# A chunked linear-attention kernel with a gated output: backward-scan decays, a Sigmoid gate, two products interleaved on opposite tiles, compact loads issued by ScalarE, no filler matmuls

## The chip, the core and the metric

One core of one Trainium2 chip runs the whole program. The metric is the device time of one execution in microseconds (us). The engines are TensorE (PE; its weight loads are listed as PEld), VectorE (DVE), ScalarE (ACT), GpSimd (POOL) and SyncE (SP). Each has its own stream of instructions and runs it in order; semaphores join the streams.

## The reference

All data are float32. There are 4 batches of 8 heads (32 units), 768 steps, head size 40. The state of a unit is a 40x40 matrix with a decay per step and column:

```
for t in range(S):
    y[:, :, t] = np.einsum('bhd,bhde->bhe', rt, state)
    Sa = np.einsum('bhde,bhe->bhd', state, at)
    state_decay = state * wt[:, :, None, :] - np.einsum('bhd,bhe->bhde', Sa, bt)
    state = state_decay + np.einsum('bhd,bhe->bhde', vt, kt)
```

The rows `y` of one step form a vector `x` of 320 numbers. A causal depthwise convolution of 5 taps over time and a sigmoid give a gate; the result is `(gate * (x @ w_val)) @ w_out`.

## The kernel before, in words

**Tiling.** Time is cut into 12 chunks of 64 steps. A tile such as `at` or `k` holds all 32 units of a chunk: the 40 components of a unit lie on partitions 0 to 39 or 64 to 103 (one parity of heads each), 16 units lie side by side, 64 steps each.

**`prep(c)`** makes the running product of the decays, `lam`, with one scan on VectorE over 1040 columns (16 units of 1 + 64; `ind` restarts the scan at each unit). Its inverse comes from Ln and Exp on ScalarE and one Newton step on VectorE (`nw0`, `nw1`, L401 and L403). `at` is multiplied by `lam`; `k` and `b` by the inverse (L406). Then come TensorE's products B-A (`mb_`, 32 matmuls, L412) and A-K (`ma_`, the same line), and the turning of `b` and `k` (L418). B-A is copied for the triangular solve (`lst0` L425, `mb` L426 on ScalarE, `lst1` L428 on VectorE), A-K is masked into `ak` (L432). The A-K products use 2 of the 4 tiles of 64x64 that TensorE's array is cut into (rows and columns of one half), the B-A products all 4.

**`tri(g)`** inverts 32x32 triangles of two chunks at once on VectorE: a transpose (L443), 60 dependent steps (L449, L452), a mask (L456), a diagonal, two transposes `dt` and `dd` (L458, L459). **`solve(c)`** joins the halves: two stages of 32 matmuls of 32x32 (`sx` L471, `sy` L477), whose moving operand is every 32nd number of `dd` or `dt`; L479 copies the triangles into `tt`, and `tt1` (L483, VectorE) adds the result of `sy`. **`gv(c)`** makes the R-V products (L494, 2 x 16 matmuls, on the other two tiles) and masks them into `mv`.

**`chain(c, hf)`** is what goes from chunk to chunk, for two halves of the units: `u0` (L511, L513), `u` (L525, L527), `g` (L538), `ys` (L552 to L556, which gives the outputs and the new state), `z` (L573), with a copy or a product by ScalarE or VectorE behind each. **`moe(c)`** is the gate and the two dense layers: GpSimd moves `y` into `xt`, ScalarE and VectorE make the convolution (L624, L628), five instructions make the sigmoid (Abs, Exp, Ln L632 to L634, L635 on VectorE, Exp L636), TensorE makes `val` (L82, L90) and `out` (L100).

**Order.** `Plan` holds every piece with an engine, an assumed duration and its dependences; a list scheduler (`order`) turns them into one fixed order for each engine, which the code then emits. At run time no engine passes over an instruction that waits. SyncE issues all loads. `k`, `b` and `w` have one buffer each, so a load waits until the chunk before has been read.

**Fillers.** While emitting, the code looks at the planned gaps of TensorE and puts dummy matmuls there (L702, 64x72 from the tile `dm`, results not read): 521 in the program. Each float32 matmul of the program appears in the trace as two, so 1042 there.

Of the kernel before, what the change touches and what calls it, by code (L numbers as in the profile page):

```python
# [109 lines left out]
def moe_steps(nc, mo, pp, wts, wz, xe, xt, store):  # L110
# [159 lines left out]
def dve(n):  # L270
    return 110 + 1.05 * n
# [6 lines left out]
def fast_path(ctx, tc, ins, out, nch, cst, wts, wz, wmx):  # L278
# [13 lines left out]
    W = new("w", [ER, P16, C + 1])  # L292
# [3 lines left out]
    Y0 = new("y0", [ER, P16, C])  # L296
# [11 lines left out]
    DD = new("dd", [128, 32, 32])  # L308
    MX = new("mx", [128, 32, 32])
# [13 lines left out]
    dm = new("dm", [128, 72])  # L323
# [7 lines left out]
    m01 = [cst[:, 224 + i:225 + i] for i in range(2)]  # L331
    plan = Plan()
# [36 lines left out]
    def load(c):  # L369
        n = c % NA  # L370
        op(("ldw", c), "SP", 700, lambda: dma(W, ins["w"][c]), w=["w"], lat=2500)
        op(("lda", c), "SP", 700, lambda: dma(AT[n], ins["a"][c]), w=[("at", n)], lat=2500)
        for x, nm in enumerate("kb"):
            op(("ld" + nm, c), "SP", 700, lambda x=x, nm=nm: dma(KB[x], ins[nm][c]), w=[nm], lat=2500)

    def load2(c):
        op(("ldvp", c), "SP", 700, lambda: dma(VP, ins["vp"][c]), w=["vp"], lat=2500)
        op(("ldvt", c), "SP", 700, lambda: dma(VT, ins["vt"][c]), w=["vt"], lat=2500)

    def load3(c):  # L380
        n = c % 2
        op(("ldrg", c), "SP", 700, lambda: dma(RG[n], ins["rg"][c]), w=[("rg", n)], lat=2500)
        op(("ldri", c), "SP", 700, lambda: dma(RI[n], ins["ri"][c]), w=[("ri", n)], lat=2800)
        op(("ldmv", c), "SP", 700, lambda: dma(MV[n], ins["mv"][c]), w=[("mv", n)], lat=2800)

    def prep(c):

        n, g = c % NA, bof[c]
        lam, at, wv = LAM[n], AT[n], W[:, :, 1:C + 1]
        lm = lam[:, :, 1:C + 1]  # L390
        op(("scan", c), "DVE", 2750, lambda: V.tensor_tensor_scan(
            out=lam.rearrange("p u t -> p (u t)"), data0=W.rearrange("p u t -> p (u t)"),
            data1=ind.rearrange("p u t -> p (u t)"), initial=0.0, op0=ALU.mult, op1=ALU.max), r=["w", "ind"], w=[("lam", n)])
# [465 lines left out]
```

## Time and profile before

| | us |
|---|---|
| median of 3 runs (630.28, 630.94, 681.89) | 630.94 |
| the profiled execution's own time | 626.14 |
| its span (first to last instruction) | 624.0 |
| TensorE busy / weight loads busy | 516.8 / 456.4 |
| VectorE busy | 422.2 |
| ScalarE busy | 223.8 |
| mean granted TensorE clock | 0.83 of 2.4 GHz |

The busy time is the union of an engine's instructions; TensorE's matmuls are pipelined, so a busy TensorE need not be at its peak. The granted clock is 1.0 (2.4 GHz) or 0.5 (1.2 GHz) at any moment; a figure between is the mean over a stretch. The chain of waits follows the work back from the last instruction, at each step to what released it.

Three stretches are spoken of. Up to about 115 us the first chunks are prepared, and the first `u` starts at 115.3 us. From 115 to 545 us all kinds of work run side by side. From 545 us on the preparations are over, and only the last chunks' chains and dense layers are left.

### The profile page before, as it was taken

The numbers are of one execution on the slowest core, as the hardware profiler recorded it, in microseconds if no ns is written. First come the engines' busy times: TensorE is split into PE (matmuls) and PEld (weight loads), VectorE is DVE, ScalarE is ACT, GpSimd is POOL, SyncE is SP. The second block draws the span as 40 slices with busy tenths as digits, with TensorE's granted clock in tenths as the row PEclk, the third lists the DMA queues.
The fourth block names the chain that finished last, engine by engine and source line by source line (L and its number), as shares of the span: only waits on it lengthen the run. The fifth ranks groups of instructions, "written<-read, shape, count | busy, mean of one in ns | idle before, by whom it ended". The sixth has DMA issues, their size and how long they took to land.

```text
span 624.0 us, 29668 instructions
## 1 busy us (share of the span) xinstructions
PE 516.8 (83%) x13715; PEld 456.4 (73%) x13715; DVE 422.2 (68%) x924; ACT 223.8 (36%) x362; POOL 74.9 (12%) x151
## 2 busy tenths in 40 slices
PE   0577889686968899878979898999899986999981
PEld 0577888586967778867877887878688885797760
DVE  6397886975883758666775868689969784342430
ACT  3114443231713423523446343455344232432230
POOL 1000000030021000300020203002030312021300
PEclk9996879777785857976986979699979897598986
DMA  8973314144054551245452636341532435001100
GB/s 209 288 180 107 91 45 107 51 141 99 3 158 114 134 163 60 54 129 160 131 149 57 175 82 185 99 126 54 164 91 74 127 95 154 23 15 32 28 22 25
DMA packets 22149, 65.59 MB, mean 105 GB/s; under 512 B 4420, under 2 KB 8508, under 8 KB 22020
## 3 DMA queue, kind: packets, MB, share of 16 engines
q1 hardware_dynamic: 14292, 55.51, 32.3%
q0 software_dynamic: 4608, 4.19, 2.6%
q10 hardware_dynamic: 3120, 3.93, 1.9%
q8 instruction: 109, 1.79, 1.2%
q14 instruction: 20, 0.16, 0.1%
HBM read 55.51 MB, written 3.93 MB: 95 GB/s over the span
## 4 chain that ended last, share of the span: by engine, by line
PE 66%; DVE 12%; DMA 10%; issue 9%; ACT 2%; SPq 0%; POOL 0%; ACTq 0%; DVEq 0%; POOLq 0%
PE pm L100 8%; PE pc L702 7%; PE pp L412 6%; PE pm L82 6%; PE pp L418 5%; PE px L471 4%; DMA b<-in_b 3%; PE px L477 3%; PE px L494 3%; PE pc L538 3%; PE pc L552 3%; PE pc L513 3%; PE pc L554 3%; PE pc L556 3%; PE pc L511 2%
## 5 line engine op out<-in xcount | busy, mean ns | idle before, releaser
L619 POOL DMA_DIRECT2D xt<-xe x144 | 73.1, 515 | 511.6 <-DVE x L452 143.3
L702 PE MATMUL pc<-dm 128*64 128x72 f32 x1042 | 94.4, 253 | 7.0 <-DVE pc L366 4.1
L702 PEld LDWEIGHTS pc<-dm 128*64 128x64 f32 x1042 | 83.4, 158 | 14.5 <-issue 5.5
L628 DVE SCALAR_TENSOR_TENSOR ag<-xt,wts,ag 128x256 f32<-128x256 f32 (+1 forms) x144 | 60.2, 437 | 14.6 <-ACT ag L624 14.6
L449 DVE TENSOR_TENSOR tm<-x 128x30 f32<-128x30 f32 (+14 forms) x210 | 68.7, 327 | 1.4
L452 DVE TENSOR_TENSOR x<-x,tm 128x30 f32<-128x30 f32 (+14 forms) x210 | 68.6, 327 | 1.3
L100 PE MATMUL pm<-wts,ag 128*128 128x320 f32 x144 | 61.1, 552 | 0.0
L554 PE MATMUL pc<-mv,kt 64*40 64x104 f32 x768 | 43.1, 259 | 2.6 <-issue 2.6
L552 PE MATMUL pc<-ri,zd 40*40 40x104 f32 x704 | 40.8, 265 | 3.6 <-issue 2.4
L100 PEld LDWEIGHTS pm<-wts,ag 128*128 128x128 f32 x144 | 27.9, 222 | 21.3 <-issue 16.7
L494 PE MATMUL px<-rg,vt 40*64 40x64 f32 x768 | 30.6, 235 | 15.4 <-DMA rg<-in_rg 15.4
L556 PE MATMUL pc<-mu,bt 64*40 64x104 f32 x768 | 42.1, 258 | 0.0
L494 PEld LDWEIGHTS px<-rg,vt 40*64 40x64 f32 x768 | 27.9, 149 | 17.4 <-issue 16.9
L406 DVE TENSOR_TENSOR b<-b,y 104x1024 f32<-104x1024 f32 x12 | 14.7, 1225 | 36.8 <-DMA b<-in_b 36.8
L525 PE MATMUL pc<-tt,u 64*40 64x64 f32 x768 | 30.9, 241 | 9.6 <-DVE tt L483 5.8
L513 PE MATMUL pc<-vp,ak 64*64 64x40 f32 x768 | 35.2, 272 | 1.9 <-issue 1.9
L525 PEld LDWEIGHTS pc<-tt,u 64*40 64x40 f32 x768 | 27.7, 131 | 12.2 <-DVE tt L483 5.9
L511 PE MATMUL pc<-st,at 40*64 40x40 f32 x704 | 32.7, 269 | 3.3 <-issue 3.3
L395 ACT ACTIVATE y<-w,bias 104x1024 f32<-104x1024 f32 x24 | 27.6, 1150 | 21.6 <-DMA w<-in_w 16.6
L412 PE MATMUL pp<-at,k 40*64 40x64 f32 x768 | 29.5, 239 | 6.1 <-DVE lst L428 3.4
L82 PE MATMUL pm<-xt,wts 128*128 128x128 f32 x192 | 34.4, 307 | 0.0
L425 ACT ACTIVATE lst<-pp,cst 128x512 f32<-128x512 f32 x12 | 13.9, 1160 | 55.9 <-PE pp L412 55.9
(104 smaller groups left out, 1070.9 us busy)
## 6 DMA issues: line engine op xcount, KB each, us to landing
mv<-in_mv SPq DMA_DIRECT2D x12, 832.0 KB
ri<-in_ri SPq DMA_DIRECT2D x12, 676.0 KB
w<-in_w SPq DMA_DIRECT2D x12, 422.5 KB
at<-in_a SPq DMA_DIRECT2D x12, 416.0 KB
b<-in_b SPq DMA_DIRECT2D x12, 416.0 KB
k<-in_k SPq DMA_DIRECT2D x12, 416.0 KB
vt<-in_vt SPq DMA_DIRECT2D x12, 416.0 KB
rg<-in_rg SPq DMA_DIRECT2D x12, 416.0 KB
```

The source lines that it names most:

```text
L82: T.matmul(out=ps[:, j * 2 * L:(j + 1) * 2 * L], lhsT=x[:, m * 128:m * 128 + 128], rhs=xt[:, q:q + 2, 4:4 + L], start=(k == 0), stop=(k == 2))
L100: T.matmul(out=ps, lhsT=gv[r, q * L:q * L + 128], rhs=wo[k][r], start=(k == 0), stop=(k == 2))
L412: T.matmul(out=PP[rows(a, 64), s, q * C:q * C + C], lhsT=KB[x][rk, 2 * q + s], rhs=at[rk, 2 * q + s], start=True, stop=True)
L449: V.tensor_tensor(out=tv, in0=XS[:, j + 1:32, j:j + 1].to_broadcast([128, n, j]), in1=XS[:, j:j + 1, 0:j].to_broadcast([128, n, j]), op=AL ...
L452: V.tensor_tensor(out=XS[:, j + 1:32, 0:j], in0=XS[:, j + 1:32, 0:j], in1=tv, op=ALU.subtract)
L494: T.matmul(out=PX[rows(a, 64), (4 * s + q) * C:(4 * s + q + 1) * C], lhsT=VT[r, m], rhs=RG[n][r, m], start=True, stop=True)
L552: T.matmul(out=o, lhsT=ZD[r, m], rhs=RI[v][r, m], start=True, stop=False)
L554: T.matmul(out=o, lhsT=KBT[0][k][r, m], rhs=MV[v][r, m], start=not c, stop=False)
L556: T.matmul(out=o, lhsT=KBT[1][k][r, m], rhs=MU[r, m], start=False, stop=True)
L619: G.dma_start(out=o, in_=x)
L628: op(("cv", c, j, k), "DVE", 90 + 1.05 * nn[k], lambda k=k, q=q, j=j: V.scalar_tensor_tensor(out=acc[:, q], in0=xt[:, q, j:j + C], scalar= ...
L702: T.matmul(out=f[0:64, 0, 440:512], lhsT=dm[:, 0:64], rhs=dm, start=True, stop=True)
```

## The change

- `prep`: Ln, Exp and the two Newton instructions go. A second scan runs backward over the same columns and gives the inverse decay times the chunk's total decay inverse, which is put into `ind` by a reciprocal of 16 columns; a memset restores `ind`. `b` is now made ahead of `k`.
- `lst`: the tile's layout is turned, so that three ScalarE copies (two of them on 32 partitions) write it in rows; `begin` now reads with a stride. The mask of `tri` moves into `dc`, one VectorE instruction per pair of chunks, which also turns the layout, so that `sx` and `sy` read rows. `dd` is transposed per chunk from `dc`. `tt1` becomes two ScalarE copies.
- `akgv(c, d)`: A-K of chunk c and R-V of chunk d alternate matmul by matmul on the four tiles. In the loop c is three chunks and d one chunk ahead of the chain. Ten calls have both; two have A-K alone, two R-V alone. `turn` holds what stood in `prep`.
- The gate is one Sigmoid; the activation table loaded at the start is another.
- `val`: 4 matmuls in place of 6 for the same columns (two of 256, two of 128).
- Loads of `vp`, `vt`, `rg`, `mv`, `ri` go from SyncE to ScalarE's queue. `mv` and `ri` are stored without their constant parts (832 to 320 KB, 676 to 416 KB) and land in pieces of 160 and 256 bytes; the identity in `ri` is loaded once per buffer.
- The fillers go. The assumed durations of the plan are changed, and so the order of everything.

The core of the diff (plan durations and host layouts are left out):

```diff
-            for k in range(3):
-                x = wv[k + j if k == 2 else k]
-                q = 8 if k == 2 else 4 * k + 2 * j
...
+        for k in range(2):
+            T.matmul(out=ps, lhsT=wv[k][:, m * 128:m * 128 + 128], rhs=xt[:, 4 * k:4 * k + 4, 4:4 + L], start=(k == 0), stop=False)
...
+    def dma2(o, i):
+        A.dma_start(out=o, in_=i)
...
-        op(("ldri", c), "SP", 700, lambda: dma(RI[n], ins["ri"][c]), w=[("ri", n)], lat=2800)
-        op(("ldmv", c), "SP", 700, lambda: dma(MV[n], ins["mv"][c]), w=[("mv", n)], lat=2800)
+        op(("ldmv", c), "ACT", 560, lambda: dma2(MV[n][:, :, C:RW], ins["mv"][c]), w=[("mv", n)], lat=LD)
+            op(("ldri", c), "ACT", 560, lambda: dma2(RI[n][:, :, 0:C], ins["ri"][c]), w=[("ri", n)], lat=LD)
...
-        op(("ln", c), "ACT", act(1024), lambda: A.activation(out=Y0, in_=lm, func=AF.Ln), r=[("lam", n)], w=["y0"])
-        op(("exp", c), "ACT", act(1024), lambda: A.activation(out=Y0, in_=Y0, func=AF.Exp, scale=-1.0), w=["y0"])
...
+        op(("rc", c), "DVE", 200, lambda: V.reciprocal(out=ind[:, :, C], in_=lm), r=[("lam", n)], w=["ind"])
+        op(("scab", c), "DVE", 2240, lambda: V.tensor_tensor_scan(
+            out=back(flat(Y0)), data0=back(WF[:, 1:P16 * (C + 1) + 1]), data1=back(flat(ind)), initial=0.0, op0=ALU.mult, op1=ALU.max),
+           r=["w", "wpad", "ind"], w=["y0"])
...
+        for x in range(2):
+            def go(x=x):
+                for q in range(8):
+                    for par in range(2):
+                        if c is not None:
+                            r = rows(par, D)
+                            T.matmul(out=PP[rows(par, 64), 0, q * C:q * C + C], lhsT=KB[0][r, 2 * q + x], rhs=AT[n][r, 2 * q + x], start=True, stop=True)
+                        if d is not None:
+                            m, r = 8 * (q // 4) + 4 * x + q % 4, rows(1 - par, D)
+                            T.matmul(out=PP[rows(par, 64), 1, q * C:q * C + C], lhsT=VT[r, m], rhs=RG[v][r, m], start=True, stop=True)
...
+        op(("dc", g), "DVE", 1150, lambda: V.tensor_tensor(
+            out=DC, in0=DT.rearrange("p t m -> p m t"), in1=maskD.unsqueeze(1).to_broadcast([128, 32, 32]), op=ALU.mult), r=["dt", "cst"], w=["dc"])
...
-        op(("tt1", c), "DVE", dve(512), lambda: V.scalar_tensor_tensor(
-            out=TT[n][:, :, 32:64], in0=pv, scalar=m01[0], in1=TT[n][:, :, 32:64], op0=ALU.mult, op1=ALU.add), r=pxb + ["cst"], w=[("tt1", n)])
+        for i in range(2):
+            lo = slice(64 * i, 64 * i + 32)
+            op(("tt1", c, i), "ACT", act(512), lambda lo=lo: A.copy(out=TT[n][lo, :, 32:64], in_=pv[lo]), r=pxb, w=[("tt1", n)])
...
-        op(("gln", c), "ACT", act(640), lambda: A.activation(out=gt, in_=gt, func=AF.Ln, bias=1.0), w=["gv"])
+        op(("gate", c), "ACT", act(640), lambda: A.activation(out=acc, in_=acc, func=AF.Sigmoid), w=ak)
...
-                for i in range(k):
-                    T.matmul(out=f[0:64, 0, 440:512], lhsT=dm[:, 0:64], rhs=dm, start=True, stop=True)
```

**The order at three places.** First, TensorE's stream at its very start. Before (L494 is R-V of chunk 0, L412 its B-A and A-K products, L702 fillers):

```order
L702 MATMUL pc_121<-dm 64x72 x5
L494 MATMUL px<-rg_86,vt 64x64 x16
L702 MATMUL pc_121<-dm 64x72 x8
L412 MATMUL pp<-at_71,b 64x64 x32
L702 MATMUL pc_121<-dm 64x72 x12
```

And now (L417 is B-A, L437 A-K, L440 R-V):

```order
L417 MATMUL pp<-at_71,b 64x64 x32
L437 MATMUL pp<-at_71,k 64x64
L440 MATMUL pp<-rg_87,vt 64x64
L437 MATMUL pp<-at_71,k 64x64
L440 MATMUL pp<-rg_87,vt 64x64
```

R-V, which needs the loads of `rg` and `vt`, stood ahead of B-A and now stands behind it.

Second, TensorE's stream in the middle of the program. Before (the rows that the trace shows from 389 to 402 us; L573 is `z`, L418 the turning of `b` and `k`):

```order
L494 MATMUL px<-rg_87,vt 64x64 x16
L702 MATMUL pc_121<-dm 64x72
L412 MATMUL pp<-at_72,k 64x64 x32
L573 MATMUL pc_121<-cst,st 40x40 x16
L573 MATMUL pc_122<-cst,st 40x40 x16
L702 MATMUL pc_121<-dm 64x72 x8
L418 MATMUL pp<-cst,b 64x40 x32
L702 MATMUL pc_122<-dm 64x72 x5
L418 MATMUL pp<-cst,k 64x40 x32
```

And now, at a like place (L95 is `out`, L500 and L503 are `sx` and `sy`):

```order
L417 MATMUL pp<-at_71,b 64x64 x32
L95 MATMUL pm<-wts,ag 128x320 x3
L500 MATMUL px<-dd,mb 32x32 x32
L95 MATMUL pm<-wts,ag 128x320 x3
L503 MATMUL px<-dc,xx 32x32 x32
L437 MATMUL pp<-at_71,k 64x64
L440 MATMUL pp<-rg_87,vt 64x64
```

The separate runs of L494 and of L412 from `k` have become one alternating run, and no dummy stands between stages.

Third, the end of the first solve. Before, VectorE's stream (L47 to L54 convert the weights, L449 and L452 are steps of `tri`, L483 is `tt1`):

```order
L51 TENSOR_SCALAR xt<-xt 128x323
L449 TENSOR_TENSOR tm<-x 128x240
L52 SCALAR_TENSOR_TENSOR wts<-xt 128x323
L452 TENSOR_TENSOR x<-x,tm 128x16x15
L483 SCALAR_TENSOR_TENSOR tt_105<-px,cst,tt_105 128x16x32
L449 TENSOR_TENSOR tm<-x 128x240
```

And now ScalarE's stream (L502 copies `xx`, L498 fills `tt` from `dc`, L425 copies `mb`, L507 is `tt1`, L538 the copy of `ut`):

```order
L502 COPY xx<-px 128x512
L498 ACTIVATE tt_106<-dc,cst 128x16x32
L425 COPY mb<-pp 128x512
L507 COPY tt_106<-px 32x16x32
L498 ACTIVATE tt_106<-dc,cst 128x16x32
L507 COPY tt_106<-px 32x16x32
L538 COPY ut_110<-pc_121 104x512
```

The last step before the first `u` has left VectorE's stream of weight conversions and triangle steps.

## Rows read from the trace of the kernel before

**Rows 1.** The three stretches: start and end, length, busy us and instructions of each engine, mean granted clock, share of the DMA engines, GB/s.

```profile
0.00:115.00 115.00, 75.26 (x1666) 71.65 (x1666) 85.28 (x171) 36.22 (x48) 1.88 (x7) 0.88 0.52 142
115.00:545.00 430.00, 379.91 (x10694) 334.46 (x10698) 313.11 (x700) 167.73 (x277) 60.93 (x120) 0.81 0.40 110
545.00:624.00 79.00, 61.64 (x1367) 50.32 (x1360) 23.78 (x55) 19.85 (x37) 12.13 (x24) 0.87 0.09 24
```

**Rows 2.** The fillers' instructions alone (L702) in the same middle stretch and in four stretches within it: busy us of PE and of PEld, granted clock, DMA share, GB/s.

```profile
115.00:545.00 430.00, 39.83 (x358) 33.05 (x358) 0.81 0.40 110
337.00:357.00 20.00, 0.00 (x0) 0.00 (x0) 1.00 0.52 140
365.00:395.00 30.00, 0.82 (x6) 0.53 (x7) 0.96 0.56 160
395.00:408.00 13.00, 4.57 (x34) 3.92 (x34) 0.50 0.43 113
425.00:457.00 32.00, 2.02 (x26) 1.57 (x24) 1.00 0.46 134
```

**Rows 3.** The chain of waits in the stretch from 115 to 545 us, by line, as shares of that stretch.

```profile
by line: issue 10.3%; PE pm L100 9.8%; PE pc L702 7.6%; PE pm L82 7.3%; PE pp L412 7.1%; PE pp L418 5.7%; PE px L471 4.6%; PE px L477 4.5%; PE px L494 4.3%; PE pc L538 4.2%; DMA b<-in_b 4.0%; PE pc L513 3.6%; PE pc L552 3.6%; PE pc L511 3.4
```

**Rows 4.** What VectorE waited for from 115 to 545 us: us in all, times, longest.

```profile
DVE b L406 <- DMA b<-in_b: 31.6, 5, 9.5
DVE tt L483 <- PE px L477: 30.8, 6, 10.7
...
DVE lst L428 <- ACT mb L426: 2.2, 3, 1.1
```

**Rows 5.** Pieces of the chain of waits between 384 and 404 us: start, length, what.

```profile
394.93 2.01 PE pc L702 x16
396.93 1.88 PE pp L418 x64
398.81 1.39 PE pc L702 x10
```

**Rows 6.** The product stages (L412 alone) in three short stretches, columns as in Rows 2: A-K at 2.4 GHz, A-K at 1.2 GHz, B-A at 2.4 GHz.

```profile
125.30:127.20 1.90, 1.90 (x64) 1.86 (x64) 1.00 0.47 75
160.00:163.60 3.60, 3.60 (x64) 3.46 (x64) 0.50 0.02 5
102.00:103.10 1.10, 1.10 (x64) 0.99 (x64) 1.00 0.79 201
```

**Rows 7.** One `sx` stage (L471 alone) at 2.4 GHz and one at 1.2 GHz, columns as in Rows 2.

```profile
419.40:421.40 2.00, 1.98 (x64) 1.82 (x64) 1.00 0.31 94
323.50:325.60 2.10, 2.02 (x64) 1.88 (x64) 0.50 0.96 245
```

**Rows 8.** Groups of VectorE's instructions by line: busy us, mean ns of one, idle before them.

```profile
L391 DVE TENSOR_TENSOR_SCAN lam<-w,ind 104x1040 f32<-104x1040 f32 x12 | 27.9, 2323 | 1.1 <-DMA w<-in_w 1.1
L403 DVE SCALAR_TENSOR_TENSOR y<-w,y 104x1024 f32<-104x1024 f32 x12 | 14.6, 1219 | 0.0
L428 DVE SCALAR_TENSOR_TENSOR lst<-pp,cst,lst 128x512 f32<-128x512 f32 x12 | 14.0, 1166 | 12.1 <-ACT mb L426 12.1
L459 DVE STREAM_TRANSPOSE dd<-x 128x1024 f32<-128x1024 f32 x7 | 13.7, 1951 | 0.0
L635 DVE SCALAR_TENSOR_TENSOR ag<-ag 128x640 f32<-128x640 f32 x12 | 9.9, 823 | 7.3 <-ACT ag L634 7.3
L443 DVE STREAM_TRANSPOSE x<-lst 128x1024 f32<-128x1024 f32 x7 | 8.8, 1253 | 0.0
L456 DVE TENSOR_TENSOR x<-x,mx 128x1024 f32<-128x1024 f32 x7 | 8.5, 1217 | 0.0
```

**Rows 9.** The DMA queues of SyncE (q1) and ScalarE (q10): packets, MB, the time of the packets as a share of 16 engines' span; and two stretches in which TensorE stood idle (busy us of PE, PEld, DVE, ACT, POOL, granted clock, DMA share, GB/s).

```profile
q1 hardware_dynamic: 14292, 55.51, 32.3%
...
q10 hardware_dynamic: 3120, 3.93, 1.9%
...
182.00:187.20 5.20, 0.21 (x7) 0.07 (x4) 3.19 (x6) 0.00 (x0) 3.50 (x7) 0.63 0.89 247
516.00:522.50 6.50, 1.07 (x74) 0.95 (x70) 4.11 (x13) 0.43 (x1) 2.70 (x6) 0.91 0.87 246
```

**Rows 10.** The timeline at the start of the program and ahead of the first `u`.

```profile
15.39 1.23 DVE L406 TENSOR_TENSOR b<-b,y 104x1024 f32<-104x1024 f32 x1
21.00 1.97 PE L494 MATMUL px<-rg,vt 40*64 40x64 f32 x32 [15.39 <-DMA rg<-in_rg]
25.01 1.75 PE L412 MATMUL pp<-at,b 40*64 40x64 f32 x64
...
96.93 1.98 PE L477 MATMUL px<-dt,xx 32*32 32x32 f32 x64
114.49 0.74 DVE L483 SCALAR_TENSOR_TENSOR tt<-px,cst,tt 128x512 f32<-128x512 f32 x1
```

**Rows 11.** Pieces of the chain of waits in the last gate and behind it.

```profile
597.48 0.75 ACT ag L632
601.41 0.77 DVE ag L644 x2
...
603.25 0.91 PE pc L702 x6
```

**Rows 12.** The timeline of ScalarE's queue: the issue of one transfer (start, length).

```profile
305.44 0.52 ACTq L651 DMA_DIRECT2D out<-xt  x1
```

More of the change, by code (lines that the diff above doesn't have):

```diff
@@ L386, in prep @@
+        if c < 2:
+            op(("eye", c), "SP", 400, lambda: dma(RI[n][:, :, C:RW], ins["eye"]), w=[("rj", n)], lat=LD)
+        if c:
+            op(("ldri", c), "ACT", 560, lambda: dma2(RI[n][:, :, 0:C], ins["ri"][c]), w=[("ri", n)], lat=LD)
     def prep(c):
         n, g = c % NA, bof[c]
[L389 to L393, printed above, removed]
@@ L405, in prep, with flat @@
-        for x, nm in enumerate("kb"):
-            op((nm + "t", c), "DVE", 90 + 1.05 * 1024, lambda x=x: V.tensor_tensor(out=KB[x], in0=KB[x], in1=Y0, op=ALU.mult), r=["y0"], w=[nm])
-        def products(x, far):
+        lam, at, wv, lm, y = LAM[n], AT[n], W[:, :, 1:C + 1], LAM[n][:, :, C], Y0[:, :, 1:C + 1]
+        def flat(x):
+            return x.rearrange("p u t -> p (u t)")
+        op(("scan", c), "DVE", 2240, lambda: V.tensor_tensor_scan(
+            out=flat(lam), data0=flat(W), data1=flat(ind), initial=0.0, op0=ALU.mult, op1=ALU.max), r=["w", "ind"], w=[("lam", n)])
@@ L409, in products @@
+        op(("ic", c), "DVE", 60, lambda: V.memset(ind[:, :, C:C + 1], WLO ** C), w=["ind"])
+        op(("at", c), "DVE", 65 + 1.05 * 1024, lambda: V.tensor_tensor(out=at, in0=at, in1=lam[:, :, 0:C], op=ALU.mult), r=[("lam", n)], w=[("at", n)])
+        for x, nm in ((1, "b"), (0, "k")):
+            op((nm + "t", c), "DVE", 65 + 1.05 * 1024, lambda x=x: V.tensor_tensor(out=KB[x], in0=KB[x], in1=y, op=ALU.mult), r=["y0"], w=[nm])
+        def products():
             for q in range(8):
                 for par, s in UNITS:
-                    rk, a = rows(par, D), par ^ s if far else par
@@ L412, in products @@
-                    T.matmul(out=PP[rows(a, 64), s, q * C:q * C + C], lhsT=KB[x][rk, 2 * q + s], rhs=at[rk, 2 * q + s], start=True, stop=True)
+                    rk = rows(par, D)
+                    T.matmul(out=PP[rows(par ^ s, 64), s, q * C:q * C + C], lhsT=KB[1][rk, 2 * q + s], rhs=at[rk, 2 * q + s], start=True, stop=True)
+        ps = PP.rearrange("p s (q t) -> p (s q) t", t=C)
+        op(("mb_", c), "PE", 1160, products, r=["b", ("at", n)], w=ppb)
+        m0 = g[1] * P16
+        op(("lst", c, 0), "ACT", act(512), lambda: A.copy(out=LST[:, m0:m0 + P16], in_=ps[:, :, 0:32]), r=ppb, w=["lst"])
@@ L442, in flat @@
             return x.rearrange("p a b -> p (a b)")
-        op(("begin", g), "DVE", 1250, lambda: V.transpose(out=flat(XS), in_=flat(LST)), r=["lst"], w=["x"])
+        op(("begin", g), "DVE", 1900, lambda: V.transpose(out=flat(XS), in_=LST.rearrange("p m t -> p t m")), r=["lst"], w=["x"])
         def step(j, half):
@@ L468, in between @@
             for m in range(P16):
                 for a in range(2):
-                    lo, hi = slice(a * 64, a * 64 + 32), slice(a * 64 + 32, a * 64 + 64)
-                    T.matmul(out=PX[hi, m * 32:m * 32 + 32], lhsT=MB[lo, k + m], rhs=DD[lo, :, o + m], start=True, stop=True)
-        def last():
-            for m in range(P16):
-                for a in range(2):
-                    lo, hi = slice(a * 64, a * 64 + 32), slice(a * 64 + 32, a * 64 + 64)
-                    T.matmul(out=PX[lo, m * 32:m * 32 + 32], lhsT=XX[hi, m], rhs=DT[hi, :, o + m], start=True, stop=True)
+                    fn(m, slice(a * 64, a * 64 + 32), slice(a * 64 + 32, a * 64 + 64), slice(m * 32, m * 32 + 32), a)
@@ L486, in gv @@
[L486 to L498 removed]
+        op(("sy", c), "PE", 1300, lambda: quad(lambda m, lo, hi, o, a: T.matmul(out=PX[lo, o], lhsT=XX[hi, m], rhs=dc[hi, m], start=True, stop=True)),
+           r=["dc", "xx"], w=pxb)
@@ L500, in chain @@
+        for i in range(2):
+            lo = slice(64 * i, 64 * i + 32)
+            op(("tt1", c, i), "ACT", act(512), lambda lo=lo: A.copy(out=TT[n][lo, :, 32:64], in_=pv[lo]), r=pxb, w=[("tt1", n)])
     def chain(c, hf):
```

196 lines of the change are left out of this document (84 added, 112 removed).

## Prediction, made before the changed kernel was run

> **What bounds the kernel now.** I read the windows first, then the chain of waits, then VectorE's waits, then single stages.
>
> The windows cut the span in three [rows 1]. Up to 115 us VectorE works 85 us and TensorE's work is largely dummies. From 115 to 545 us TensorE is busy 380 of 430 us (88%), VectorE 313 (73%), ScalarE 168 (39%). Of TensorE's 380 us, 40 are fillers [rows 2], so 340 are work. The middle is what decides, and TensorE is its fullest engine.
>
> The chain of waits of the middle agrees [rows 3]: nearly every line in it is TensorE's. Fillers alone have 7.6% of 430 us, 33 us. Two places show how: the pieces from 395 to 400 us are a run of fillers, a stage, another run of fillers and the next stage, without a wait [rows 5]. TensorE takes its stream in order, so a dummy planned into a gap that has closed delays real work.
>
> VectorE is the second bound. It idles 430 - 313 = 117 us in the middle, and 33 of these are waits for `sy` in `tt1` (30.8) and for ScalarE's copy in `lst1` (2.2) [rows 4]. The change gives both pieces of work to ScalarE; on VectorE, what stands behind them in the stream waits too.
>
> **The change, part by part.** The sum goes against the profiled execution: span 624.0 us, own time 626.14, which is 0.8% under the median of 630.94 (factor 1.0077).
>
> *Fillers.* Gone from the chain of the middle: -33 us. At least half of that should come, since another wait can end last in some gaps; at most all of it.
>
> *A-K and R-V.* A stage of 32 A-K matmuls on two tiles takes 1.90 us at 2.4 GHz and 3.60 at 1.2, one of 32 B-A matmuls on four tiles 1.10 [rows 6]. R-V is of the same size and on two tiles like A-K. So a pair goes from about 3.8 to 2.2 us if alternating on opposite tiles gives B-A's rate, 42% less. On the chain, R-V (L494) has 4.3%, 18.5 us, and A-K its part of L412's 30.5 us, 1.90 to 1.10 against B-A, 19.3 us [rows 3, 6]. 42% of 37.8 is 16; not all calls have both products, so -15. Bounds: 0, if the alternating order overlaps no better than two tiles do, and -16.
>
> *`sx` and `sy`.* A stage takes 1.98 us at 2.4 GHz and 2.02 at 1.2 [rows 7], so the array's clock does not set it; what is peculiar to it is a moving operand of every 32nd number. That becomes contiguous. No row shows a contiguous one. From below: half the columns of an A-K stage on two tiles, 0.95; from above 1.98. VectorE's transposes of 1024 numbers cost 1951 ns with such a stride and 1253 without [rows 8]; 1.98 divided by the same 1.56 is 1.27, which I take. L471 and L477 have 9.1% of the chain, 39 us [rows 3]; 36% of it is -14. Bounds 0 and -20. [...]
>
> *The clock.* Against the gains stands what the dummies did for the granted clock, 0.81 in the middle, so 38% of the time at 1.2 GHz [rows 1]. The rows say that the kind of work decides more than the dummies: from 337 to 357 us the clock stayed at 1.0 with no filler, and from 365 to 395 at 0.96 with 6; from 395 to 408, with turning, `u0` and 34 fillers, it was 0.50 [rows 2]. I take 0.76, ten points more time at 1.2 GHz; product stages take 1.9 times as long there, others less, so work on TensorE slows by about 5%, and with some 220 us of TensorE left on the chain that is +10 us. Bounds: 0, and the last rival. [...]
>
> *VectorE as a check.* Removed: two Newton instructions of 14.6 each (L403; its twin has the same size), L428 14.0, L459 13.7, L635 9.9, L456 8.5 [rows 8], `tt1` 12 x 0.74 = 9 [rows 10]; 85 us. Added: a backward scan like the forward one, 27.9; twelve half-size transposes, half of 1253 ns each, 8; seven `dc` between 1217 ns, a plain product (L456) [rows 8], and twice 1166 ns, taken at 1.95 us as a strided transpose, 14; `begin` with a stride, 7 x 0.7 = 5; reciprocals and memsets, at most a quarter of a plain product each, 12 x 0.3 = 4. Sum 59, net -26; were a backward scan half as fast, +28 more. The middle holds 74% of VectorE's work, so 313 becomes 294, and its idle time 117 - 33 = 84, as the copies pass to ScalarE. That is 378 us, and the TensorE sum, 430 - 33 - 15 - 14 + 10 = 378, meets it. ScalarE can carry it: five more issues a chunk at 0.52 us [rows 12], two small copies more, five long passes fewer; at +5 us a chunk it would be 218 of 378 us.
>
> *Loads.* `mv` and `ri` send half the bytes in 2048 + 1664 pieces a chunk. The nearest rows are ScalarE's packets: 1.9% of 16 x 624 us over 3120 packets, 61 ns for 1.26 KB; SyncE's take 226 ns for 3.9 KB [rows 9]. At 61 ns the pieces take 14 us of 16 engines a chunk, at bytes alone 2.7, against 5.5 now. DMA engines are busy 40% of the middle [rows 1]; at the upper bound that becomes about 70%. The loads have two buffers and more than a chunk's time, so I cost them at nothing; that cover gone, `b` waits longer: its 4.0% of the chain, 17 us, could double or, with the assumed load time now longer in the plan, go. TensorE's long stops at 182 to 187 and 516 to 522 us, with nothing to wait for, came while the DMA engines were 87 to 89% busy [rows 9]: such bursts may shorten or lengthen, within the same 17 us.
>
> *Start and end.* R-V stood first in TensorE's stream and waited for `rg` until 21.0 us, so B-A began at 25.0, though `b` was ready at 16.6 [rows 10]: -8 us. The first `sy` ended at 98.9, but `tt1` came at 114.5 behind VectorE's steps; on ScalarE it comes at once, and since VectorE's work stays I take -6 of 15.6. So -14, bounds -8 and -23. At the end, the gate from 597.5 to 601.4 becomes one pass of 0.75 us, -3, and fillers of 0.9 us go [rows 11]: -4, bounds -3 and -7.
>
> *Sum.* Middle -52, start -14, end -4: -70, span 554, own time 556, median 556 x 1.0077 = **560 us**. With the bounds of the four middle terms one at a time the figure moves by up to 17 either way.
>
> **The rivals.**
>
> *Half kept.* The order stays a fixed list, and A-K of chunk c+3 now stands in one stage with R-V of chunk c+1. `ys` of c+1 thus waits for a load and a preparation two chunks further on. For it: `b` was late five times, by up to 9.5 us [rows 4]. Against: the load time assumed by the plan is longer. Price: those 31.6 us once more, on the state's way: 560 + 32 = 592, range 590 to 612.
>
> *More.* VectorE's 84 us of idle time that the sum keeps in the middle shrink too, since TensorE, which it mostly waits for, is less full: a third gone is 28 less, 532, and with `sx` and the start at their bounds 517.
>
> *The change does little.* The copies and loads moved to ScalarE hold up `u0`, `ut` and `ze`, which stand behind them in one stream; a load that waits for `ys` blocks them. The fillers' time is then waited instead of filled, and the gain of the products goes the same way: -33 and -15 fail, and +15 of stalls come: about 624. Against it: ScalarE is busy only 39%.
>
> *Slower.* The granted clock of the middle falls so far that TensorE's work fills it. 340 us of work at 38% half-rate are, with 1.7 as the mean ratio, 340 x (0.62 + 0.38/1.7) = 287 us at full rate; 25 less by the edits, 262. All at half rate that is 445 us; at 88% busy the middle takes 506, 76 more than now: span 624 + 76 - 18 = 682, median 689. It decides from a granted clock of about 0.6 in the middle: there 262 us of work take 394, and the middle 448, so that nothing is gained. For it: 0.50 from 395 to 408 us; against: 0.96 to 1.00 for 82 us with 32 fillers.
>
> **How the numbers follow.** Forecast as summed (525 to 590, centre 560) 0.65; half kept (590 to 612) 0.16; more (under 525) 0.06; little change (612 to 644) 0.07; slower 0.06. A measurement of this kernel tells about 2% from no change, 618 to 644 being the same. So faster 0.88, same 0.06, slower 0.06. The range 520 to 610 leaves out about 0.05 below and 0.14 above.
>
> **What would show it.** Right: a first `u` near 100 us; a middle near 380 us with VectorE at 75 to 80%; no L483-like wait on VectorE; pairs of 2.2 us and `sx` of 1.3 us; a granted clock of 0.72 to 0.85. Wrong: a clock under 0.6; VectorE idle for `b` or `k` over 40 us; ScalarE's copies waiting behind issues; `sx` still at 2 us; a scan that is longer backward than 2.3 us.

## The result, and the profile after

The changed kernel takes 598.29 us (median of four; 588.70 to 603.05) against 632.58 us for the kernel before on the same chip; the ratio is 0.938, 95% interval 0.921 to 0.955. Executions of one kernel spread by 0.2 to 8% here, so a ratio with an interval leaves out those over 1.5% above the fastest of their kernel (two of these four), a median takes all, and the profiles of `first_small_late`, `start_fixed` and `best` are of such longer executions. The changed kernel is faster, but the forecast of 560 us was 38 us too low (33 by the ratio). The execution in the profile took 588.70 us, with a span of 586.9, against 626.14 and 624.0 before. Stretches are read inside one profiled execution, totals by their intervals.

I cut both spans at the start of the first `u` matmul and at that of chunk 10 (the 1281st of the 1536 records of `u`). First the kernel before: start and end of the stretch, length, busy us of PE, PEld, DVE, ACT and POOL with instructions, granted clock, DMA share, GB/s.

```profile
0.00:115.30 115.30, 75.27 (x1668) 71.66 (x1668) 85.58 (x172) 36.22 (x48) 1.88 (x7) 0.88 0.52 142
115.30:544.10 428.80, 379.00 (x10662) 333.55 (x10664) 311.91 (x696) 167.73 (x277) 60.93 (x120) 0.81 0.40 110
544.10:624.00 79.90, 62.54 (x1392) 51.22 (x1391) 24.68 (x58) 19.85 (x37) 12.13 (x24) 0.86 0.09 25
```

The changed kernel, same view:

```profile
0.00:120.70 120.70, 39.43 (x1149) 36.51 (x1152) 84.96 (x179) 30.56 (x50) 1.88 (x7) 1.00 0.49 116
120.70:506.80 386.10, 321.39 (x10039) 273.71 (x10031) 289.41 (x664) 138.79 (x265) 60.94 (x120) 0.78 0.41 100
506.80:586.90 80.10, 58.33 (x1402) 45.35 (x1401) 25.90 (x63) 16.14 (x35) 12.13 (x24) 0.83 0.13 37
```

The start became 5.4 us longer (forecast 14 shorter), the middle 42.7 shorter (forecast 52), the end stayed (forecast 4 shorter). So 19 of the 33 us that are missing on the profiled execution lie in the start. In the middle TensorE fell from 88% busy to 83%: it now stands idle 64.7 us there (386.10 less 321.39), VectorE 96.7 (386.10 less 289.41).

The start of the changed kernel, from its timeline (start, length, engine; ACTq and SPq are the issues of transfers):

```profile
6.39 11.91 ACTq L332 DMA_DIRECT2D mv<-in_mv  x2
14.98 1.98 PE L417 MATMUL pp<-at,b 40*64 40x64 f32 x64 [14.98 <-DVE b L411]
18.34 9.32 ACTq L332 DMA_DIRECT2D ri<-in_ri  x2
26.96 7.13 SPq L329 DMA_DIRECT2D ri<-in_eye  x2
30.19 0.56 ACT L421 COPY lst<-pp 128x512 f32<-128x512 f32 x1
32.06 1.97 DVE L469 STREAM_TRANSPOSE x<-lst 128x1024 f32<-128x1024 f32 x1 [8.12 <-ACT lst L424]
34.23 3.35 SPq L329 DMA_DIRECT2D w<-in_w  x1
```

B-A runs at 14.98, 10 us earlier than before [rows 10], as forecast. But ScalarE stands in four issues of small pieces from 6.39 to 27.66 (3.8 us of it between the first two) and copies `lst` only at 30.19; `begin`, the transpose L469 that opens the first triangle, starts at 32.06. SyncE issues `w` of chunk 1 at 34.23, behind the identity loads.

The stages came out as costed. A-K and R-V alternating, then one `sx` at a granted clock of 0.50 and one at 1.00 (each line alone in a short stretch: L437, then L440, then L500; busy us of PE and PEld, granted clock, DMA share, GB/s):

```profile
239.55:240.85 1.30, 1.15 (x32) 1.02 (x32) 1.00 0.00 0
...
239.55:240.85 1.30, 1.16 (x32) 1.02 (x32) 1.00 0.00 0
```

```profile
396.50:398.60 2.10, 1.92 (x64) 1.78 (x64) 0.50 0.25 70
426.10:427.40 1.30, 1.20 (x64) 1.09 (x64) 1.00 0.91 226
```

A half stage of 32 + 32 matmul records takes 1.16 us, a pair 2.3 (forecast 2.2). `sx` takes 1.20 (forecast 1.27) at a granted clock of 1.00 and 1.92 at 0.50: with a contiguous operand it follows the clock, which it did not before, at 1.98 and 2.02 [rows 7].

What VectorE waited for in the middle, 120.7 to 506.8 us (us in all, times, longest):

```profile
DVE ak L443 <- PE pp L440: 12.7, 5, 8.5
DVE st L571 <- PE pc L565: 11.5, 9, 5.1
DVE b L411 <- PE pc L520: 11.2, 2, 6.2
DVE mu L549 <- ACT lst L424: 9.2, 1, 9.2
...
DVE b L411 <- DMA b<-in_b: 7.9, 3, 6.9
```

The two large waits of before, 31.6 us for `b` and 30.8 for `sy` [rows 4], are down to 7.9 and gone from VectorE. In their place stand many smaller ones, for TensorE's and ScalarE's stages.

### The profile page after: what moved, and what is told of

Its sections match the earlier page's. It is cut to its first block, busy times and chain, and to the rows that moved or that the text cites. A ratio compares the mean times of both kernels' runs of the same rounds, so it can differ in the third digit from the quotient of the medians.

```text
span 586.9 us, 27337 instructions
## 1 busy us (share of the span) xinstructions
PE 419.1 (71%) x12577; PEld 355.6 (61%) x12577; DVE 400.3 (68%) x905; ACT 185.5 (32%) x350; POOL 75.0 (13%) x151
## 3 DMA queue, kind: packets, MB, share of 16 engines
q8 instruction: 100, 1.64, 1.2%
## 4 chain that ended last, share of the span: by engine, by line
PE 51%; DVE 19%; DMA 16%; issue 10%; ACT 2%; POOL 1%; ACTq 0%; SPq 0%; DVEq 0%; POOLq 0%
PE pm L95 7%; DMA b<-in_b 5%; PE pp L460 5%; PE pp L437 4%; PE pc L547 3%; DMA xt<-xe 3%; PE pc L563 3%; PE pc L565 3%; PE pc L561 3%; PE pm L76 3%; PE px L503 3%; DMA mv<-in_mv 3%; PE pc L534 3%; DVE tm L475 3%; DMA out<-xt 3%
## 5 line engine op out<-in xcount | busy, mean ns | idle before, releaser
L95 PE MATMUL pm<-wts,ag 128*128 128x320 f32 x144 | 66.8, 596 | 2.4 <-ACT xt L655 1.6
L437 PE MATMUL pp<-at,k 40*64 40x64 f32 x768 | 36.6, 258 | 36.9 <-ACT mb L425 15.7
L417 PE MATMUL pp<-at,b 40*64 40x64 f32 x768 | 21.9, 284 | 50.9 <-DVE b L411 47.5
L437 PEld LDWEIGHTS pp<-at,k 40*64 40x64 f32 x768 | 33.0, 168 | 39.8 <-ACT mb L425 15.8
L417 PEld LDWEIGHTS pp<-at,b 40*64 40x64 f32 x768 | 19.7, 193 | 52.9 <-issue 27.9
L95 PEld LDWEIGHTS pm<-wts,ag 128*128 128x128 f32 x144 | 29.8, 237 | 27.1 <-issue 18.3
L401 ACT ACTIVATE dp<-w,bias 104x1024 f32<-104x1024 f32 x24 | 27.6, 1149 | 44.0 <-DMA mv<-in_mv 25.7
L536 PE MATMUL pc<-u,tt 64*64 64x40 f32 x768 | 36.5, 267 | 1.6 <-issue 1.6
L536 PEld LDWEIGHTS pc<-u,tt 64*64 64x64 f32 x768 | 34.9, 181 | 2.0 <-issue 1.9
L549 DVE TENSOR_TENSOR mu<-pc,cst 128x512 f32<-128x512 f32 x24 | 16.5, 687 | 28.5 <-PE pc L547 12.8
L522 PEld LDWEIGHTS pc<-vp,ak 64*64 64x64 f32 x768 | 31.9, 181 | 5.5 <-ACT zd L585 2.3
L534 PEld LDWEIGHTS pc<-tt,u 64*40 64x40 f32 x768 | 33.6, 153 | 2.0 <-issue 2.0
```

Of the source, the lines that this page charges most:

```text
L95: T.matmul(out=ps, lhsT=gv[r, q * L:q * L + 128], rhs=wo[k][r], start=(k == 0), stop=(k == 2))
L437: T.matmul(out=PP[rows(par, 64), 0, q * C:q * C + C], lhsT=KB[0][r, 2 * q + x], rhs=AT[n][r, 2 * q + x], start=True, stop=True)
L522: T.matmul(out=o, lhsT=AKM[k][rows(par, 64), m], rhs=VP[rows(par, 64), m], start=True, stop=not c)
L534: T.matmul(out=ps[rows(1 - a, D), 1, j * C:j * C + C], lhsT=u0[r, j], rhs=TT[t][r, m], start=True, stop=True)
L536: T.matmul(out=ps[r, 0, j * D:j * D + D], lhsT=TT[t][r, m], rhs=u0[r, j], start=True, stop=True)
```

## The experiments

In the table "first u" and "middle" are cut as above; all numbers of one row are from one profiled execution, the median from all executions; "clock" is the granted clock of the middle. The ratio is to the kernel before on the same chip, which took 625 to 633 us; where no interval is given it is the ratio of the medians.

| run | first u | middle | clock | median us | to before |
|---|---|---|---|---|---|
| before | 115.3 | 428.8 | 0.81 | 632.6 | 1 |
| changed | 120.7 | 386.1 | 0.78 | 598.3 | 0.938 (0.921 to 0.955) |
| changed, again | 119.9 | 389.4 | 0.77 | 590.2 | 0.939 (0.930 to 0.949) |
| before_no_filler | 123.3 | 416.4 | 0.77 | 627.0 | 1.003 |
| after_filler | 118.8 | 384.3 | 0.81 | 584.7 | 0.935 |
| long_tensor | 121.8 | 394.9 | 0.79 | 608.1 | 0.969 (0.959 to 0.978) |
| less_tensor | 120.3 | 388.4 | 0.76 | 586.0 | 0.933 (0.927 to 0.940) |
| less_vector | 120.3 | 391.8 | 0.75 | 592.8 | 0.945 (0.936 to 0.955) |
| double_scan | 126.8 | 393.0 | 0.75 | 592.9 | 0.945 (0.938 to 0.952) |
| first_small_late | 113.0 | 391.5 | 0.77 | 584.1 | 0.934 |
| first_small_gpsimd | 117.9 | 383.3 | 0.78 | 577.3 | 0.923 |
| start_fixed | 110.4 | 392.5 | 0.76 | 582.9 | 0.929 |
| b_two | 108.9 | 388.2 | 0.78 | 576.2 | 0.920 (0.913 to 0.927) |
| best | 102.8 | 389.7 | 0.76 | 573.7 | 0.905 (0.897 to 0.913) |

The control was the changed kernel once more:

> The changed kernel as it is, beside the three that follow: both theories expect 0.92 to 0.955 of the kernel before, a first u at 119 to 122 us and 380 to 392 us from the first u to that of chunk 10.

**The fillers**, left out of the kernel before (`range(k)` becomes `range(0)`), and put back into the changed one by the old rule (`TS`, `GAP`, `TH`, `WIN` and the loop over `k`).

> The kernel before, with the filler matmuls left out and nothing else: this part of the change alone. Theory (fillers were 33 us of the chain of the middle and buy little clock): 598 to 610 us, against 633 for the kernel before, and a granted clock of 0.74 to 0.80 in the middle. Rival 1 (the gaps they filled are then waited out): 622 to 633 us with TensorE idle 30 us more in the middle than now without fillers. Rival 2 (the clock falls): granted clock under 0.68 in the middle, 630 us or more.

> The changed kernel with fillers put back by the same rule as before (406 of them in place of 521, on a constant tile as operand): this part of the change undone. Theory (TensorE now stands idle 65 us of the middle, waiting with VectorE in turns, so fillers fall partly into real waits): 605 to 618 us in place of 598, with the clock up by 0.03 or less. Rival 1 (each filler delays work as in the kernel before): 625 to 635. Rival 2 (the fillers' clock is worth what they cost): 593 to 601, granted clock in the middle 0.85 or more.

The kernel before without fillers, the three stretches:

```profile
0.00:123.30 123.30, 39.61 (x1088) 37.43 (x1088) 85.75 (x172) 36.00 (x48) 1.88 (x7) 1.00 0.50 132
123.30:539.70 416.40, 357.57 (x10304) 316.61 (x10304) 311.20 (x694) 167.06 (x277) 60.89 (x120) 0.77 0.40 113
539.70:622.30 82.60, 57.88 (x1286) 45.43 (x1285) 25.37 (x60) 20.07 (x38) 12.13 (x24) 0.79 0.09 24
```

Taking only the fillers out wins 12.4 us in the middle, loses 8.0 in the start and 2.7 at the end: nothing in sum. TensorE's work without fillers rose in the middle, from 379.00 less some 40 us of fillers [rows 2], 339, to 357.57: about 18 us more (an estimate) for the same matmuls at a clock of 0.77 in place of 0.81, and idle time from 49.8 to 58.8. Put back, they cost nothing either: 384.3 us in the middle, total ratio 0.935. The theory of 33 us falls in both runs. Rival 1 of the first has the total right, though TensorE's idle time grew by 9 us and not by 30; rival 2 of the second is right that fillers cost nothing, though the clock only came to 0.81.

**TensorE's other edits undone** in the same order (the edit in short):

```diff
-for q in range(8): for par in range(2): A-K(q, par); R-V(q, par)
+for z in range(2): for q in range(8): for par in range(2): A-K if z == 0; R-V if z == 1
-sx: rhs=DD[lo, m]            sy: rhs=dc[hi, m]
+sx: rhs=DDS[lo, :, m]        sy: rhs=DCS[hi, :, o + m]    (strides 16 and 32)
```

> The changed kernel with two of its TensorE edits undone inside the same order: in each stage all A-K matmuls come first and then all R-V ones, and sx and sy read a moving operand with a stride (16 and 32 numbers; the numbers are other ones than sx and sy need, so the output is not the reference's). From the two traces this should put 20 to 28 us of TensorE's work back into the stretch from the first u to that of chunk 10 (386 us). Theory T (that stretch is set by TensorE's work): it takes 404 to 414 us, and the kernel 18 to 30 us more than the changed one. Theory V (it is set by VectorE and the hand-overs, since TensorE stands idle 65 us of it): 386 to 395 us, and the kernel at most 10 us more.

The middle of the control and of this run, and one `sx` of this run (L503 alone, granted clock 1.00):

```profile
119.90:509.30 389.40, 326.03 (x10038) 276.26 (x10031) 289.72 (x664) 138.73 (x265) 61.15 (x120) 0.77 0.41 99
121.80:516.70 394.90, 337.65 (x10034) 290.23 (x10030) 289.38 (x661) 138.70 (x265) 61.17 (x120) 0.79 0.41 98
...
234.00:236.00 2.00, 1.98 (x64) 1.82 (x64) 1.00 0.37 106
```

With the stride back, `sx` takes 1.98 us again in place of 1.20, so the stride was what set it. The run put 11.6 us of busy time back on TensorE, not the 20 to 28 expected. Between the theories: by the ratios it costs 0.029 of 627 us, 18 us with an interval of about 8 either way (theory T's lower end); by the profiled execution, the shortest of its four, 5.5 us of the middle and 6 in all (theory V). Two of the forecast's terms, 29 us together, are thus worth 6 us by the one and 10 to 27 by the other.

**Less work on one engine**, where it is not in the state's way: `out` makes `k in ((0,), (0, 2))[j]` in place of `range(3)`, and taps `j < 3` in place of `j < 5`.

> The changed kernel with half of the matmuls of the output projection left out (so that the output lacks those terms), in the same order: about 25 us less of TensorE's work from the first u to that of chunk 10. Theory T: that stretch takes 358 to 368 us in place of 386. Theory V: 376 to 388.

> The changed kernel with two of the four convolution taps on VectorE left out (the output lacks those terms), in the same order: about 23 us less of VectorE's work from the first u to that of chunk 10. Theory V: that stretch takes 362 to 372 us in place of 386. Theory T: 378 to 388.

The middle of `less_tensor`:

```profile
120.30:508.70 388.40, 306.01 (x9985) 267.44 (x9977) 289.75 (x664) 137.97 (x265) 61.14 (x120) 0.76 0.40 99
```

and that of `less_vector`:

```profile
120.30:512.10 391.80, 329.01 (x10041) 282.18 (x10035) 275.20 (x610) 138.55 (x265) 60.88 (x120) 0.75 0.41 98
```

TensorE loses 20 us of busy time against the control (326.0) and the middle only 1.0; VectorE loses 14.5 (289.7, less than the 23 I expected) and the middle gains nothing. Theory T falls with the first run, theory V with the second.

What took the place of the 20 us can be read in TensorE's waits. The profile calls it `issue` when an engine stands idle and nothing is shown that it waits for: 42.7 us of TensorE's idle time in the control's middle, 55.3 in that of `less_tensor`.

**More work on VectorE**: the backward scan twice (`lambda: scan` becomes `lambda: (scan, scan)`).

> The changed kernel with every backward scan run twice (the second writes the same numbers): 2.32 us more on VectorE in each chunk, between the load of w and the product b, in the same order; nothing else. Theory V (the preparation of a chunk on VectorE is on the way of the middle, which is why the shorter preparation brought time although TensorE and VectorE both idle): the stretch from the first u to that of chunk 10 grows by 14 to 20 us from 386 to 389, and the kernel by 18 to 28 us from 590. Rival (VectorE's 97 us of idle time in that stretch take it up, as they did when convolution taps were left out): at most 4 us more in the stretch, at most 8 in the kernel.

Its middle holds 307.33 us of VectorE's work and is 3.6 us longer than the control's:

```profile
126.80:519.80 393.00, 335.06 (x10041) 283.23 (x10033) 307.33 (x672) 138.83 (x265) 61.11 (x120) 0.75 0.41 98
```

The rival holds in the middle: 17.6 us more work are taken up by idle time. In the start, though, 4 scans of 2.32 us (9.3) put the first `u` off by 6.1 to 6.9 us.

**The start.** First the small loads alone, later (`late` = the loads `mv`, `ri` and `eye` of chunks 0 and 1, put behind `("mb", 1)` in the list), or from GpSimd (`(G if c < 2 else A).dma_start`); `ri` of chunk 2, early in ScalarE's queue too, stays.

> The changed kernel, with only the first loads in small pieces (mv of chunks 0 and 1, ri of chunk 1, and the two loads of the identity columns) issued later: behind ScalarE's copy mb of chunk 1 in place of ahead of its first copies. Theory A (the start lost because ScalarE's queue stands about 21 us in these issues before it can copy lst, and w of chunk 1 waits behind the identity loads and behind relu): begin of the first triangle starts at 19 to 22 us in place of 32.1, the first u at 106 to 112 us in place of 120.8, and the kernel takes 584 to 592 us in place of 598. Rival (VectorE's own work and the single buffer of b set the first u, so that an early begin only waits later): begin is as early as in theory A, but the first u stays at 117 to 121 us and the kernel at 595 to 600.

> The changed kernel, with mv of chunks 0 and 1 and ri of chunk 1 issued by GpSimd at the same place in the list; the identity loads stay with SyncE. The traffic stays, only ScalarE's queue is free. Theory A (the queue was what was blocked): ScalarE's first relu starts before 9 us and begin at 18 to 23 us; the first u comes at 108 to 115 us, total 587 to 594. Rival (the issues were slow because the transfers themselves filled the DMA engines, so that b, cst or w come late whoever issues them): begin at 27 us or later, first u 117 to 123 us, total 596 to 602.

With the small loads late (timeline):

```profile
6.75 1.03 ACTq L332 DMA_DIRECT2D ri<-in_ri  x1
16.71 0.58 ACT L421 COPY lst<-pp 128x512 f32<-128x512 f32 x1 [6.29 <-PE pp L417]
19.23 8.03 SPq L329 DMA_DIRECT2D w<-in_w  x1
22.33 0.33 DVE L44 TENSOR_SCALAR ag<-ag 128x323 int32<-128x323 int32 x1 [3.79 <-DMA ag<-in_wts]
23.93 1.90 DVE L469 STREAM_TRANSPOSE x<-lst 128x1024 f32<-128x1024 f32 x1
```

and from GpSimd:

```profile
17.38 1.99 PE L417 MATMUL pp<-at,b 40*64 40x64 f32 x64 [17.38 <-DVE b L411]
19.49 0.59 ACT L421 COPY lst<-pp 128x512 f32<-128x512 f32 x1 [9.60 <-PE pp L417]
24.10 9.10 SPq L329 DMA_DIRECT2D ri<-in_eye  x2
27.68 0.33 DVE L44 TENSOR_SCALAR ag<-ag 128x323 int32<-128x323 int32 x1 [3.47 <-DMA ag<-in_wts]
29.28 1.89 DVE L469 STREAM_TRANSPOSE x<-lst 128x1024 f32<-128x1024 f32 x1
```

Both free ScalarE's queue: `lst` is copied 13.5 and 10.7 us earlier. But `begin` gains 8.1 us in the one and 2.8 in the other, because a second hold appears: six conversions of weights stand ahead of it in VectorE's order and wait for the weights (the first, L44, runs at 22.33, as in the changed kernel at 22.26). In the GpSimd run, where the small pieces still travel, weights and `b` land later, by 5.4 and 2.4 us. So theory A is half right for the late loads, and in the GpSimd run its rival (full DMA engines) has `begin` and the first `u` right. The first `u` came 7.7 and 2.8 us earlier; the totals, 584.1 and 577.3 us, do not follow that order, and no run says why. With GpSimd as the issuer the DMA engines were about as full up to 30 us, 86% busy against 88% in the changed kernel, and `b` came 2.4 us later (B-A at 17.38, against 14.98 with ScalarE as the issuer).

Then the conversions moved behind the sixth step of the first triangle:

> The run with the first small loads issued later, and in addition the six conversions of weights that stood ahead of begin on VectorE (they waited for the weights until 22 us) put behind the sixth step of the first triangle. Theory A (lst is ready at 18.5 us and nothing but the order on VectorE holds begin): begin at 18 to 20 us in place of 23.9 there and 32.1 in the changed kernel, the first u at 104 to 110 us in place of 113.0 and 120, and the kernel 10 to 16 us under the changed one. Rival (w of chunk 1, which was on its way until 32 us, and b's single buffer set what comes next): first u 111 to 115, kernel as with the first small loads late.

```profile
16.70 0.59 ACT L421 COPY lst<-pp 128x512 f32<-128x512 f32 x1 [6.86 <-PE pp L417]
17.89 1.03 SPq L329 DMA_DIRECT2D ri<-in_eye  x1
18.70 1.94 DVE L469 STREAM_TRANSPOSE x<-lst 128x1024 f32<-128x1024 f32 x1
```

`begin` is at 18.70 as theory A says, 13.4 us earlier than in the changed kernel, and the first `u` at 110.4, 10.3 earlier, just outside its 104 to 110. The rest went to `w` of chunk 1 and to waits for `b`, as the rival says. (`w` still stood right behind a load of the identity columns in SyncE's queue.)

**Two buffers for b** (`KB[1]` becomes `BB[c % 2]`; same order), and both together:

> The changed kernel with two buffers for b in place of one, in the same order (the room for it: the scratch output of relu becomes bf16, xx shares the tile of dd, and dd of the last chunk stands a little later). Theory H (in the chain the wait for b, which can be loaded only when the buffer is turned, is 15 us up to the first u and 8 to 14 us in the middle, and it comes off): the first u at 104 to 112 us in place of 120, the stretch from there to the u of chunk 10 at 374 to 382 in place of 386 to 389, ratio to the kernel before 0.90 to 0.925. Rival (w or the triangle of the batch takes its place): first u 116 to 121, stretch 384 to 390, ratio 0.93 to 0.945.

> Both together: small loads late, begin ahead of the conversions, two buffers for b. If A and H hold and add up: first u at 90 to 100 us, stretch 374 to 382, ratio to the kernel before 0.87 to 0.905. If only A holds: first u 104 to 110, ratio 0.91 to 0.925. If one limit stands behind both: 0.92 to 0.94.

VectorE's longest waits in the middle of `best`, where `b` has two buffers:

```profile
DVE mu L553 <- PE pc L551: 26.5, 7, 8.2
DVE dd L503 <- PE px L507: 15.2, 3, 7.7
DVE st L575 <- PE pc L569: 13.1, 9, 5.0
```

Theory H holds in the start (first `u` 11.8 us earlier) and fails in the middle: the waits for `b` are gone, and the middle stays at 388 to 390 us, with longer waits for `g` (L551) and `sy` (L507), and with 53.6 us of TensorE's `issue` stops in `b_two` and 46.4 in `best` against 42.7 in the control. `best` brings the first `u` to 102.8, 17.9 us earlier than the changed kernel, at a ratio of 0.905 (0.897 to 0.913) against 0.939 (0.930 to 0.949). It beats both kernels, with a first `u` between the two bands that I had given.

## Why the prediction was right or wrong

- **Direction: right.** Faster, inside the range of 520 to 610, but in the band of the rival "half kept" (590 to 612). That rival's mechanism is not what happened: waits of VectorE for `b`'s load in the middle fell from 31.6 to 7.9 us, and TensorE stood idle ahead of the paired stages for 2.3 us in all there. That the time fell into this band is chance.
- **Start, -14 forecast, +5.4 measured: the step that failed most.** B-A did start 10 us earlier and `tt1` did come at once behind `sy`. What failed is the term for the loads, costed at nothing because buffers and a chunk's time cover them, and the price of an issue, 0.52 us taken from a late, single one [rows 12]. Ahead of the first copies four issues hold ScalarE 21 us. I had this mechanism as a rival for the middle ("the change does little") and not for the start. Undoing it alone gives 7.7 us of the first `u` back, with the order on VectorE 10.3; a second buffer for `b`, which the kernel before had not either, brings it to 17.9. So 10.3 of the 19.4 us are traced. The fillers' removal, 8.0 us in the kernel before and 1 to 2 in the changed one, may have a share in the rest.
- **Fillers, -33, and the clock, +10: wrong.** Net 23 forecast, 12 measured in the middle of the kernel before, nothing in total. A share of the chain is no gain by itself: without them TensorE's other work takes about 18 us longer, it idles 9 us more, and the start is 8.0 us longer. I gave the start no term for the fillers. In the changed kernel they change nothing: 0.935 with them, 0.938 and 0.939 without.
- **Pairs, -15, and `sx`/`sy`, -14: the stages right, the gain too large.** 2.3 and 1.20 us against 2.2 and 1.27; undone together they cost 6 us (profile) or 10 to 27 (times).
- **VectorE's work: right.** 294 forecast for the middle, 289.4 measured. The backward scan costs 2318 ns, as the forward one, and the strided `begin` and `dc` 1953 and 1920 ns against 1.95 assumed:

```profile
L398 DVE TENSOR_TENSOR_SCAN lam<-w,ind 104x1040 f32<-104x1040 f32 x12 | 27.8, 2318 | 0.1
L405 DVE TENSOR_TENSOR_SCAN y<-w,ind 104x1040 f32<-104x1040 f32 x12 | 27.8, 2318 | 0.0
L469 DVE STREAM_TRANSPOSE x<-lst 128x1024 f32<-128x1024 f32 x7 | 13.7, 1953 | 8.2 <-ACT lst L424 8.1
L484 DVE TENSOR_TENSOR dc<-dt,cst 128x1024 f32<-128x1024 f32 x7 | 13.4, 1920 | 0.0
```

- **The middle, -52 forecast, -42.7 measured: nearly right for a wrong reason.** I added up what leaves TensorE's chain, and let VectorE's sum confirm it. The runs show that neither sum sets this stretch: it stays within 384 to 393 us with 20 us less on TensorE, 14 less or 18 more on VectorE, fillers or none, one buffer for `b` or two. Of the 42.7 us, the fillers explain 12 by the kernel before and nothing by the changed one, and TensorE's edits 5.5 by the one profile; the rest must come from what I gave no gain of its own (`tt1` and `lst` on ScalarE, the shorter preparation, the new order and load times), and no run separates these.
- **What sets the middle stays open.** Several readings fit. In one, TensorE and VectorE wait for each other in turns, so that relieving one alone gives nothing; against it, only 19 of TensorE's 64.7 idle us are shown as waits for VectorE. In another, the chain of a chunk's state stages sets it, each late by what stands ahead of it in its queue: from `u` of chunk 10 to that of chunk 11, where no chunk is prepared any more, a chunk takes 23.6 us, in the middle 38.6 on average (25.7 from chunk 3 to 4, 68.6 from chunk 6 to 7). A third, GpSimd's moves and the stores, has 24 us in the chain of the changed kernel's middle.
- **A term that the prediction put at nothing: `issue`.** It stands first in [rows 3], 10.3%, where I read "nearly every line is TensorE's", and it is the largest entry in the chain of the changed kernel's middle too, 44 us; below it, the queue of the kind `instruction` (packets, MB, share of 16 engines):

```profile
by line: issue 11.3%; PE pm L95 8.4%; PE pp L460 4.8%; PE pc L547 4.4%; PE px L503 4.1%; PE pc L565 4.0%; PE pc L563 3.8%; DMA xt<-xe 3.7%; PE pc L534 3.7%; PE pc L561 3.6%; DMA b<-in_b 3.6%; PE pm L76 3.3%; PE pp L437 3.3%; PE px L500 3.1%
...
q8 instruction: 100, 1.64, 1.2%
```

  Of TensorE's 64.7 idle us, 41.7 are such stops. All 23 of 0.9 us or more end 1.28 to 1.59 us after the end of a 16 KB packet of q8, though only a fifth of the middle lies 0.9 to 1.9 us behind one; in the kernel before it is all 18, 1.25 to 1.75 us. The queue's 1.64 MB are 65 bytes for each of some 25 thousand instructions of TensorE. So these look like waits of TensorE for its own instructions, and they grew where TensorE or `b` was relieved. This is read from the times alone: fewer and longer matmuls would test it, as relieving both engines at once, shortening `ys`, or leaving out the moves would test the other readings; none of it was run.
- **End, -4 forecast, +0.2 measured.** The missing 4 us were not followed up.

## What to carry to other kernels

Price an issue at the place where it stands: at the start of this program the first load of 2048 pieces of 160 bytes was issued in 0.68 us, but four issues that stood behind a load in small pieces on their queue held their engine 6.05 to 8.03 us each while the DMA engines were 89 to 99% busy, so here such a load belongs behind the first copies and behind the loads that they need. A share of the chain is no gain by itself: the fillers' 33 us brought 12 in their stretch and nothing in all. Take a piece out of the kernel before by itself, or add work to an engine, before its busy time is called the bound. Where a stretch doesn't move when either engine is relieved, the gain is to be looked for elsewhere, here in the start.

## What the runs showed of the hardware that was not expected

- At the start of the changed kernel, with the DMA engines 94% busy from 6 to 28 us, ScalarE's first `mv` issue (128 x 16 x 40 numbers) took 0.68 us and the second, behind it on the same queue, 7.40:

```profile
6.39 0.68 ACTq L332 DMA_DIRECT2D mv<-in_mv  x1
10.89 7.40 ACTq L332 DMA_DIRECT2D mv<-in_mv  x1
```

  Of the two loads' 4096 pieces of 160 bytes, 494 had started by 18 us. At 54.4 us in the run with late loads, in a stretch with the DMA engines 51% busy (30 to 60 us), the two took 0.64 and 1.25 us. SyncE's issue of `w`, not in small pieces, took 8.03 us at 19.2 in that run, right behind a load of the identity columns (1664 pieces) and with the engines 90% busy (6 to 28 us), but in `best`, with no such load ahead, 0.31:

```profile
19.61 0.31 SPq L333 DMA_DIRECT2D w<-in_w  x1
```

  In the kernel before, SyncE's issue of `vp` at 14.78 us took 0.33 us with the engines full (share 1.00 from 14 to 21 us). So full engines alone did not make an issue long here. The long ones, 7.40 and 7.82 us (`mv`, `ri`), 6.05 (identity) and 3.35 (`w`) in the changed kernel and 8.03 (`w`) in the run with late loads, stood behind a load in small pieces on their queue, with the engines 89% busy or more; at 72% a second `ri` load behind the first took 1.47.
- Without fillers the profile shows a granted clock of 1.00 for the whole start, yet B-A takes 1.98 us there, as against 1.10 with fillers, at the same reading of 1.00 [rows 6], and as long as later at 0.50 (L417 alone in the changed kernel):

```profile
385.60:387.60 2.00, 1.97 (x64) 1.78 (x64) 0.50 0.12 41
```

  Where the column reads 1.00 the duration of a known stage has to be looked at too.
- With fillers the granted clock of the middle is 0.81, without them 0.77 in the kernel before and 0.77 to 0.78 in the changed one. The other runs lie between 0.75 and 0.79, with 0.75 both where VectorE lost work and where it got more, so a difference of 0.02 shows nothing.
